# An attention block in which one shifted copy of VectorE's exponentials is made by accumulating DMA transfers

## The chip, the cores and the metric

The kernel runs on one core of one Trainium2 chip. Its time is the device time of one launch, in microseconds (us). Five engines work side by side: PE (TensorE, matmuls), ACT (ScalarE), DVE (VectorE), POOL (GpSimd) and SP (SyncE, which here only issues DMA transfers). Each engine has its own queue and runs it in order; they wait for one another through semaphores.

## The reference

Multi-head attention with 16 heads of 28 columns, for one sequence of 2048 positions and a width of 448, in bf16:

```python
qkv = (x @ wqkv).reshape(B, S, 3, H, Dh).transpose(2, 0, 3, 1, 4)
q, k, v = qkv[0], qkv[1], qkv[2]
scores = einsum("bhqd,bhkd->bhqk", q, k) * (Dh ** -0.5)
p = softmax(scores, axis=-1)
o = einsum("bhqk,bhkd->bhqd", p, v)
return o.transpose(0, 2, 1, 3).reshape(B, S, D) @ wo
```

## The kernel before, in words

**Tiling.** The 16 heads form 4 groups `g` of 4, a head taking 32 partitions. The 2048 queries form 4 chunks `c` of 512. A pair (g, c) is a set, so there are 16 sets, and in each set every head has 16 key tiles of 128 keys: 64 steps a set, 1024 in all. In a step PE multiplies keys by queries into 128x512 scores in PSUM (L706), an engine takes their exponential, and PE multiplies the values by it into the set's bank `o` (L994). A ones column in V gives the softmax's denominator. When a set is complete, VectorE copies `o` to `o_sb` (L1023), SyncE gathers the denominators into `den`, VectorE takes reciprocals (L1032), SyncE scatters them to DRAM (`scr`) and spreads them over partitions (`rr`, L1042), and POOL multiplies `o_sb` by `rr` (L1045). The output projection follows for a chunk that has all four groups.

**Two ways to the exponential.** ACT takes two steps at a time from a pair of banks (`a0`, `a1`): one 128x1024 Exp into a bf16 tile `pt` (L898; ten such tiles, NPT). VectorE takes one step at a time from a bank `d0`, `d1` or, when free, `m`. Scores come scaled by 128 times log2 e, so that adding a constant and storing int16 gives the bits of a bf16 number near the exponential (L913, tile `I`). Its error is averaged out by two further copies, the same integers plus 43 and plus 85 (SHIFT), `J1` and `J2`, which meet copies of V scaled by 201/256 and 159/256. Four VectorE steps form a chain: one `I` tile of 128x2048, and when it is complete, VectorE adds 43 and then 85 to the whole tile (two instructions of L936). So a step of VectorE has three value matmuls, and one of ACT's has one.

**The order.** All instructions are written out by a planner that runs when the kernel is built (`pick_pe`, `pick_act`, `pick_dve`, `pick_pool`, `pick_sp`). It keeps a time for each engine, takes the engine that is free first and gives it the best work that is ready by planned durations and latencies; each engine's queue has that order on the chip. PE puts scores first, then value matmuls in waves of four (one for each head) and side jobs: projections of K, Q and V for later groups, norms and output projections. A job has a priority, a gate (the step from which it may run), needs, and a landing time if it is a DMA. `urgent` lifts K and Q jobs of the next group when fewer than URGENT steps are left before it. If the queue of recent work is thin, PE gets a matmul of zeros (`dense`).

**VectorE's share.** `d_more` gives VectorE a step whenever it has a free bank and `dve_ok` finds that VectorE will be done by the time ACT runs out of what is left; otherwise ACT takes it. A chain opens for the current set, or for the next one when the current set has fewer than 2*DRAIN steps left. There may be NCH = 3 chains with value matmuls still to come.

**POOL and VectorE.** `port` keeps a planned POOL job and a planned J pass (or other VectorE pass from SBUF to SBUF) apart, and `after_shared` makes each POOL job wait for the last such VectorE pass ahead of it in the plan. POOL has no job that waits for a DMA other than the row scaling, and no transfers behind the head.

**Side jobs that the change touches.** `k_job` and `kn_job` (keys and their largest norm), `q_job` (a query chunk, and the SP transfers of its rows into QP, L448), `qn_job` (a bound from the query norms, two VectorE passes `z` and `su`, L502 and L505, and its SP transfers, L513), `v_job` (V projection in two parts), `oproj_job` (output rows through `osb`). Group 0 takes its weights from `WG`, two small tiles of their own; `offs` is a constant tile of two rows which SP copies into all QP tiles at the start (L184).

Of the kernel before, what the change touches and what calls it, by code (L numbers as in the profile page):

```python
# [12 lines left out]
I16 = mybir.dt.int16  # L13
# [11 lines left out]
URGENT = 100  # L25
# [3 lines left out]
class Op:  # L29
    def __init__(self, eng, dur, emit, need=(), gives=(), pri=0, acq=None, rel=None, gate=0, lag=0.0, land=0.0,  # L30
                 cols=0, port=False):
        self.eng, self.dur, self.emit = eng, dur, emit
        self.need, self.gives, self.pri = list(need), list(gives), pri
        self.acq, self.rel, self.gate, self.lag, self.land, self.cols, self.port = acq, rel, gate, lag, land, cols, port
# [3 lines left out]
def kernel(  # L38
# [35 lines left out]
    NCH = 3  # L74
    DRAIN = 8
# [20 lines left out]
    WG = [big.tile([CK, CC, HG * Dh + WPAD], BF16, name=f"WG{t}") for t in range(2)]  # L96
# [31 lines left out]
    def load_w0(t, eng):  # L128
        eng.dma_start(out=WG[t][:], in_=wq3[:, :, t * D:t * D + HG * Dh + WPAD])
# [33 lines left out]
    offs = const.tile([2, QW], BF16, name="offs")  # L163
# [12 lines left out]
    nc.vector.memset(offs[:], OFFS)  # L176
# [4 lines left out]
    for z in range(2):  # L181
        for c in range(NQC):
            for k in range(2):
                nc.sync.dma_start(out=QP[c][k][z][HP * k + Dh + NQC - 1 - c:P:2 * HP, :], in_=offs[:])  # L184
# [67 lines left out]
    def run(op, t):  # L252
        op.emit()
        if op.eng == "PE":
            note(t, op.cols)
        end = t + op.dur
        if op.eng == "PE" and main_on():
            cur["c_end"] = end
        if op.port:
            port[op.eng] = end  # L260
        for n in op.gives:
            evt[n] = (end + op.land, op.eng)
        if op.acq is not None:
            res[op.acq] = None
        if isinstance(op.rel, tuple):
            parts.setdefault(op.rel[0], []).append(end + LATS.get((op.eng, "PE"), LAT))
            if len(parts[op.rel[0]]) == op.rel[1]:
                res[op.rel[0]] = max(parts.pop(op.rel[0]))
        elif op.rel is not None:
            res[op.rel] = end + LATS.get((op.eng, "PE"), LAT)  # L270
        ops[op.eng].remove(op)
        return end
# [59 lines left out]
    def kn_job(g, bank, pri, gate=0):  # L332
        key = ("KN", g)

        def mm(sc):
            if sc == 0:
                held[key] = bank_tile(bank) if bank[0] != "a" else pair_tile(bank)
            quarters(held[key][:, 0:QW], maskK[:, sc, :], sqt.pop(("K", g, sc))[:], sc == 0, sc == NQC - 1)

        def red():  # L340
            kst[g] = wk.tile([P, 1], F32, name="kst")
            nc.vector.reduce_max(out=kst[g][:], in_=held.pop(key)[:, 0:QW], axis=AX.X)

        def spread_rows():
            a = wk.tile([P, HP], F32, name="kbc")
            nc.vector.tensor_copy(out=a[:], in_=kst[g][:].to_broadcast([P, HP]))
            b = wk.tile([P, HP], F32, name="kbt")
            nc.vector.transpose(out=b[:], in_=a[:])
            kmt[g] = wk.tile([P, 1], F32, name="kmt")
            cur["shared"] = nc.vector.reduce_max(out=kmt[g][:], in_=b[:], axis=AX.X)  # L350

        for sc in range(NQC):
            add("PE", D_WAVE, lambda sc=sc: mm(sc), pri=pri, gate=gate, cols=512,
                need=[("ksq", g, sc)] + ([("KNp", g, sc - 1)] if sc else []), gives=[("KNp", g, sc)],
                acq=bank if sc == 0 else None)
        add("DVE", 0.61, red, need=[("KNp", g, NQC - 1)], gives=[("kst", g)], rel=bank, pri=pri)
        add("DVE", 0.65, spread_rows, need=[("kst", g)], gives=[("km", g)], pri=pri, port=True)
# [66 lines left out]
    def q_job(g, c, bank, pri, gate=0, split=2):  # L424
# [9 lines left out]
        def evac():  # L434
            if first:
                t = qtt[0] = wk.tile([P, QW], BF16, name="qt0", bufs=1)
            else:
                t = QAt[(g, c)] = big.tile([P, QW], BF16, name=f"QA{c}", tag=f"QA{c}", bufs=1)
            if first:
                nc.vector.tensor_scalar(out=t[:], in0=held[key][:, 0:QW], scalar1=qmask[:, 0:1],  # L440
                                        scalar2=qoff[:, 0:1], op0=ALU.mult, op1=ALU.add)
            else:
                nc.vector.tensor_copy(out=t[:], in_=held[key][:, 0:QW])  # L443
# [12 lines left out]
        if first:  # L456
            add("ACT", 0.62, lambda: act_square(key, qmask), need=[key + (split - 1,)], gives=[("qsq", g, c)],
                rel=(bank, 2), pri=pri)
        else:
            add("POOL", 1.08, lambda: square(key, QAt[(g, c)][:]), need=[key], gives=[("qsq", g, c)], pri=pri, port=True)  # L460
            add("SP", 2.4, rows, need=[key, ("QZ", c, g % 2)] + ([("Oset", ORDER.index((g - 2, c)))] if g > 1 else []),
                gives=[("QR", g, c)], land=1.6, pri=1)
# [29 lines left out]
    def qn_job(g, cs, bank, pri, gate=0):  # L492
# [15 lines left out]
        def place():  # L508
            su = held.pop(("su",) + key)
            for c in cs:  # L510
                for k in range(2):
                    r = slice(HP * k + Dh + c, P, 2 * HP)
                    nc.sync.dma_start(out=QP[c][k][g % 2][r, :], in_=su[r, :])  # L513

        for k in range(len(cs)):
            add("PE", D_WAVE, lambda k=k: mm(k), pri=pri, gate=gate, cols=512,
                need=[("qsq", g, cs[k]), ("km", g)] + ([key + (k - 1,)] if k else []), gives=[key + (k,)],
                acq=bank if k == 0 else None)
        add("DVE", 0.88, bound, need=[key + (len(cs) - 1,)], gives=[("su",) + key], rel=bank, pri=pri, port=True)
        add("SP", 1.2 * len(cs), place, need=[("su",) + key] + [("QR", g, c) for c in cs],  # L520
            gives=[("QA", g, c) for c in cs], land=1.4, pri=1)

    def v_job(g, b, t0, bank, pri, gate=0, eng="DVE"):

        key = ("V", g, b, t0)
        n = XB if g is not None else XB // 2
        g0, g1 = (g, g + 1) if g is not None else (GH, G)
        w = (g1 - g0) * HG * Dh

        def mm(part):  # L530
            if part == 0:
                held[key] = bank_tile(bank)
            for u in range(part * n // 2, (part + 1) * n // 2):
# [15 lines left out]
        for p in range(2):  # L549
            add("PE", 4 * 0.1 if g is None else 8 * 0.065, lambda p=p: mm(p), pri=pri, gate=gate, cols=4 * 196,  # L550
                need=[("XT", b, 0), ("XT", b, 1), ("W", 2)] + ([key + (p - 1,)] if p else []), gives=[key + (p,)],
                acq=bank if p == 0 else None)
        add(eng, 0.53 if eng == "DVE" else 0.5, evac, need=[key + (1,)],
# [12 lines left out]
    def oproj_job(c, tq, pri):  # L566
# [8 lines left out]
        def evac():  # L575
            held[key + ("sb",)] = osb = wk.tile([P, D], BF16, name="osb", bufs=4)
# [9 lines left out]
        add("DVE", 0.535, evac, need=[key + (1,)], gives=[key], rel="m", pri=pri)  # L586
        add("SP", 0.4, store, need=[key], gives=[key + ("st",)], pri=9)
# [62 lines left out]
    for g in range(1, G):  # L650
# [4 lines left out]
        jobs += [lambda gt, c=c: q_job(g, c, "m", 100 * g + 10 + c, gt) for c in range(NQC)]  # L655
        jobs += [lambda gt: qn_job(g, list(range(NQC)), "m", 100 * g + 20, gt)]
# [20 lines left out]
    chain = {"cur": None, "used": 0}  # L677
# [70 lines left out]
    def dve_ok(t, k):  # L748
        if chain["cur"] is None and chain["used"] >= NCH:
            return False  # L750
        if chain["cur"] is not None and half_left(chain["cur"]["s"], 0) != half_left(chain["cur"]["s"], 1):
            return True
        fin = max(free["DVE"], t + 0.5) + 0.62 * (len(a_fifo) + k + 1) + 1.4 + (1.2 if adds else 0.0)
# [30 lines left out]
    def d_more(s, t, acting):  # L784
        got, taken = [], []
        for b in d_banks(t):
# [8 lines left out]
            if ch is None:  # L795
                chain["used"] += 1
                ch = chain["cur"] = {"I": wk.tile([P, HG * QW], I16, name="I4", bufs=NCH), "s": step[0], "n": 0,
                                     "open": 0, "next": 0, "done": 0}
# [111 lines left out]
    def do_a(t):  # L910
# [6 lines left out]
        ch["open"] += NTERM  # L917
        ch["done"] += 1
        pending.append({"step": step, "k": 0, "ap": dst.bitcast(BF16), "ready": end + LATS[("DVE", "PE")], "pt": None, "ch": ch})
        if ch["done"] == HG:  # L920
            adds.append([ch, HG, 1])
        else:
            flush()
        return end

    def flush():
        ch = chain["cur"]
        if ch is not None and ch["done"] == ch["n"] and not any(remain[ch["s"]]):
            chain["cur"] = None
            adds.append([ch, ch["n"], 1])  # L930

    def do_add(t):
        ch, m, k = adds[0]
        w = slice(0, m * QW)
        r = ch[k] = wk.tile([P, HG * QW], I16, name=f"J{k}", bufs=NCH)
# [16 lines left out]
    def pv_cands(t):  # L952
# [6 lines left out]
        for e in pending:  # L959
            if e["step"][0] == s and e["ready"] <= t:  # L960
                v = v_time(e)
                if v is not None and v <= t:
                    out_.append(e)
        return out_
# [14 lines left out]
    def do_pv(t, ws):  # L979
# [9 lines left out]
        for w in ws:  # L989
# [7 lines left out]
            for e in w:  # L997
# [5 lines left out]
                else:  # L1003
                    e["ch"]["open"] -= 1
                    if e["ch"]["open"] == 0 and e["ch"] is not chain["cur"] and e["ch"]["done"] == e["ch"]["n"]:
                        chain["used"] -= 1
# [4 lines left out]
    def finish_set(s, end):  # L1011
# [9 lines left out]
        def evac():  # L1021
            st["o_sb"] = wk.tile([P, QW], F32, name="o_sb")
# [16 lines left out]
        def spread():  # L1039
            scr = st["scr"]  # L1040
            st["rr"] = wk.tile([P, QW], F32, name="rr")
# [6 lines left out]
        add("DVE", 0.61, evac, need=[("Oset", s)], gives=[("osb", s)], rel="o", pri=-5)  # L1048
        add("SP", 0.6, gather, need=[("osb", s)], gives=[("den", s)], land=1.5, pri=2)
        add("DVE", 0.16, recip, need=[("den", s)], gives=[("rec", s)], pri=50, lag=2.0, port=True)  # L1050
        add("SP", 0.35, scatter, need=[("rec", s)], gives=[("scr", s)], land=1.1, pri=2)
        add("SP", 0.5, spread, need=[("scr", s)], gives=[("rr", s)], land=7.0, pri=2)
# [21 lines left out]
    def urgent(op):  # L1074
        n = op.gives[0]
        if n[0] not in ("K", "KNp", "Q", "QN") or n[1] == 0:
            return False
        first = min(k for k in range(NSET) if ORDER[k][0] == n[1])
# [52 lines left out]
    def pick_dve(t):  # L1131
        flush()
        op, nxt = best("DVE", t)
        can_add = adds and port["POOL"] <= t
# [6 lines left out]
        if op is not None:  # L1141
            return run(op, t), None
        if a_fifo and a_fifo[0][0] <= t:
# [4 lines left out]

    def pick_pool(t):
        op, nxt = best("POOL", t)  # L1150
        if op is not None:
# [92 lines left out]
    for tq in rest:  # L1244
# [4 lines left out]
        osb = wk.tile([P, D], BF16, name="osb", bufs=4)  # L1249
# [35 lines left out]
```

## Time and profile before

| what | value |
|---|---|
| median of 3 runs | 366.55 us (366.45 to 366.99) |
| profiled execution | 366.38 us, its span 364.6 us |
| first and last exponential of L898 start | 19.0 us, 355.2 us |
| J passes (L936): shortest, median, longest | 630, 686, 1401 ns |
| copies of `o` (L1023), one a set | 44.5 us the first, 337.2 us the last |
| ACT waits of PE for a score bank (L706 behind L898) | 10.0 us in 29 waits |
| PE waits for QP rows by DMA | 0.8 us in 2 waits |
| mean DMA rate over the span | 34 GB/s |

The span runs from the first to the last instruction; the time of an execution has a little around it. In a row of a group stand the line, engine, operation, output and input, shapes and count, then the busy time, the mean of one alone, the idle time just before such instructions and what ended it.

### The profile page before, as it was taken

How to read it: one execution, taken by the hardware profiler on the slowest of the kernel's cores; microseconds unless marked ns; L12 is line 12 of the kernel's file. 1: busy time of each engine (PE TensorE's matmuls, PEld its weight loads, DVE VectorE, ACT ScalarE, POOL GpSimd, SP SyncE). 2: the span in 40 equal slices, each digit the busy share in tenths (PEclk: the TensorE clock that was granted, in tenths of full speed). 3: DMA queues.
4: the chain of work that ended last, by engine and by line, in shares of the span. 5: the costliest groups of instructions: out<-in, count | busy, mean ns of one | idle time of the engine just before them, and what ended most of it. 6: DMA issues, size and time to landing. Idle time of an engine off the chain costs nothing.

```text
span 364.6 us, 10984 instructions
## 1 busy us (share of the span) xinstructions
PE 346.3 (95%) x4515; PEld 115.5 (32%) x4515; DVE 343.8 (94%) x646; ACT 347.7 (95%) x381; POOL 68.0 (19%) x103
## 2 busy tenths in 40 slices
PE   8999999999999999999999999998998999999995
PEld 4433233332333333332222322222322232222233
DVE  7789998999999999999999998999999999999993
ACT  4789999999999999999999999999999999999992
POOL 8941113013102212212012223101010010101010
PEclk9999999999999999999999999999999999999999
DMA  8520100001110000011000001100000001010111
GB/s 238 141 46 15 28 14 22 4 32 24 31 34 30 4 5 31 17 31 39 18 16 3 31 10 37 43 19 13 4 30 3 32 13 55 16 60 24 41 44 52
DMA packets 15050, 12.30 MB, mean 34 GB/s; under 512 B 6808, under 2 KB 13080, under 8 KB 15000
## 3 DMA queue, kind: packets, MB, share of 16 engines
q1 hardware_dynamic: 13448, 10.18, 9.9%
q10 hardware_dynamic: 1040, 1.02, 0.9%
q8 instruction: 35, 0.57, 0.7%
q0 software_dynamic: 512, 0.40, 0.5%
q14 instruction: 15, 0.12, 0.1%
HBM read 7.58 MB, written 1.96 MB: 26 GB/s over the span
## 4 chain that ended last, share of the span: by engine, by line
PE 53%; ACT 32%; issue 7%; DVE 6%; DMA 1%; DVEq 0%; ACTq 0%
ACT pt L898 32%; PE a L706 20%; PE o L994 15%; PE m L282 7%; PE m L289 7%; DVE I L913 2%; DVE J L936 1%; DMA xs<-in_x_dram 1%; PE a L282 1%; PE d L282 1%; DVE QA L443 0%; PE o L738 0%; PE d L289 0%; PE d L706 0%; ACT L146 0%
## 5 line engine op out<-in xcount | busy, mean ns | idle before, releaser
L898 ACT ACTIVATE pt<-a 128x1024 bf16<-128x1024 f32 x366 | 336.4, 1186 | 1.7 <-PE d L706 0.8
L913 DVE TENSOR_SCALAR I<-d 128x512 int16<-128x512 f32 x264 | 173.4, 683 | 7.3 <-PE d L706 6.5
L706 PE MATMUL a<-QP,KA 32*128 32x512 bf16 (+1 forms) x720 | 140.9, 381 | 11.4 <-ACT pt L898 10.0
L994 PE MATMUL o<-pt,V 128*32 128x512 bf16 x732 | 107.2, 384 | 0.1
L936 DVE TENSOR_SCALAR J<-I 128x2048 int16<-128x2048 int16 x146 | 98.5, 699 | 0.3
L706 PEld LDWEIGHTS <-KA 32*128 32x128 bf16 (+1 forms) x1041 | 51.0, 91 | 149.4 <-issue 146.5
L706 PE MATMUL d<-QP,KA 32*128 32x512 bf16 (+1 forms) x259 | 85.7, 384 | 0.0
L994 PE MATMUL o<-J,V 128*32 128x512 bf16 x584 | 79.0, 384 | 0.0
L994 PE MATMUL o<-I,V 128*32 128x512 bf16 x292 | 66.4, 385 | 0.2
L994 PEld LDWEIGHTS <-V 128*32 128x32 bf16 x1608 | 29.4, 94 | 48.9 <-issue 45.9
L1045 POOL TENSOR_TENSOR xs<-o_sb,rr 128x512 bf16<-128x512 f32 x12 | 15.3, 1273 | 107.6 <-DVE J L936 80.1
L282 PE MATMUL m<-XT,WRAW 112*32 112x512 bf16 x384 | 29.8, 384 | 0.0
L304 POOL TENSOR_TENSOR sq<-QA 128x512 bf16<-128x512 bf16 x15 | 15.6, 1040 | 57.6 <-DVE QA L443 28.7
L304 POOL TENSOR_TENSOR sq<-KA 128x512 bf16<-128x512 bf16 x12 | 12.5, 1039 | 60.0 <-DVE KA L322 34.8
L913 DVE TENSOR_SCALAR I<-m 128x512 int16<-128x512 f32 x28 | 19.1, 683 | 0.0
L289 PE MATMUL m<-WRAW,XT 112*32 112x112 bf16 (+1 forms) x768 | 18.1, 230 | 0.0
L1045 POOL TENSOR_TENSOR OTL<-o_sb,rr 128x512 bf16<-128x512 f32 x3 | 3.8, 1272 | 57.5 <-DVE J L936 57.5
L289 PEld LDWEIGHTS <-XT 112*32 112x32 bf16 x768 | 11.7, 96 | 8.1 <-issue 8.1
L289 PE MATMUL m<-WO,xs 128*32 128x448 bf16 x156 | 12.1, 358 | 0.0
L1023 DVE COPY o_sb<-o 128x512 f32<-128x512 f32 x15 | 10.3, 686 | 0.9 <-PE o L994 0.6
L289 PE MATMUL m<-sq,maskK 128*32 128x512 bf16 x108 | 10.8, 388 | 0.3 <-DVE QA L443 0.2
L706 PE MATMUL m<-QP,KA 32*128 32x512 bf16 (+1 forms) x28 | 10.8, 384 | 0.0
(113 smaller groups left out, 192.1 us busy)
## 6 DMA issues: line engine op xcount, KB each, us to landing
rr<-scr SPq DMA_DIRECT2D x15, 256.0 KB
QP<-QA SPq DMA_DIRECT2D x60, 28.0 KB
out_dram<-osb SPq DMA_DIRECT2D x12, 112.0 KB
WRAW<-in_wqkv_dram SPq DMA_DIRECT2D x3, 392.0 KB
xs<-in_x_dram ACTq DMA_DIRECT2D x4, 224.0 KB
xs<-in_x_dram SPq DMA_DIRECT2D x4, 224.0 KB
QP<-su SPq DMA_DIRECT2D x32, 2.0 KB
out_dram<-pt SPq DMA_DIRECT2D x2, 224.0 KB
```

Source lines behind the costliest of these rows:

```text
L282: nc.tensor.matmul(out=ps[HP * i:HP * (i + 1), :], lhsT=w[:, cc, h * Dh:h * Dh + HP], rhs=XT[c][cc // 2][:, cc % 2, :], start=(cc == 0), s ...
L289: nc.tensor.matmul(out=out[r, :], lhsT=lhsT[:, r], rhs=rhs, start=start, stop=stop, tile_position=(0, HP * i), **k)
L304: after_shared(nc.gpsimd.tensor_tensor(out=t[:], in0=src, in1=src, op=ALU.mult))
L706: nc.tensor.matmul(out=out_ap, lhsT=KAt[(g, j // XB)][r, (j % XB) * P:(j % XB + 1) * P], rhs=q[r, :], start=(n == 0), stop=(n == len(terms ...
L898: nc.scalar.activation(out=pt[:], in_=ps[:], func=ACT.Exp, scale=LN2 / 128.0)
L913: nc.vector.tensor_scalar(out=dst, in0=pd[:], scalar1=BIAS, scalar2=0.0, op0=ALU.add, op1=ALU.max)
L936: cur["shared"] = nc.vector.tensor_scalar(out=r[:, w], in0=ch["I"][:, w], scalar1=float(SHIFT[k]), scalar2=None, op0=ALU.add)
L994: nc.tensor.matmul(out=o[HP * i:HP * (i + 1), :], lhsT=VT[e["k"]][g, j // XB][:, j % XB, HP * i:HP * (i + 1)], rhs=e["ap"], start=(SETMM[k ...
L1023: nc.vector.tensor_copy(out=st["o_sb"][:], in_=o[:])
L1045: m = nc.gpsimd.tensor_tensor(out=otile(g, c), in0=st["o_sb"][:], in1=st["rr"][:], op=ALU.mult)
```

## The change

**J1 of an early chain by DMA.** If a chain opens with at least FAR = 30 steps left in its set, and the set isn't the first (FIRST = 1), it is "far": POOL fills its `J1` tile with 43 in every int16 ahead of time (a memset of 128x1024 int32 words), and when the chain's `I` is complete, POOL issues a DMA transfer that adds `I` to `J1` (`accum_op=ALU.add`). VectorE's first J pass is left out for it; the pass for `J2` stays. Other chains keep both passes. The plan has 1.05 us for the fill, 0.88 for the issue and ACC_LAND = 5.6 for the landing, and for 1.5 us behind the planned landing PE takes such blocks last.

**Buffers.** `I4` has four tiles (NCH), `J1` four (NJ), `J2` three (NCH2), each with a test of its own on what has used it; before, all three had three. Room comes from `WG` (now in the `rr` and `o_sb` buffers), `offs` (now in a `pt` tile, an exponential's), `qt0` (now in `z`), one `rr` instead of two, three `osb` instead of four, and one `kbc` and `kbt` each.

**The plan.** SyncE's transfers get longer landings (QP rows 4.0 for later groups where 1.6 stood, bounds 5.0 for 1.4, `den` 3.0 for 1.5, `rr` 8.0 for 7.0, output stores 5.0). DRAIN is 10 instead of 8. V jobs have four parts instead of two and count as urgent (URGENT_V); URGENT is 130; the later part of a started job counts as urgent. The bound job of group 1 is split, chunk 0 by itself; transfers of bounds are planned chunk by chunk. A chain that has waited AGE = 2.5 for its J pass goes ahead of passes from PSUM, and POOL may give way to it once in 3 us.

```diff
-URGENT = 100
+URGENT = 130
+URGENT_V = 40
...
-    NCH = 3
-    DRAIN = 8
+    NCH = 4
+    NCH2 = 3
+    NJ = 4
+    FAR = 30
+    FIRST = 1
+    AGE = 2.5
+    SPLITQ = {1: ([0], [1, 2, 3]), 2: ([0, 1, 2, 3],), 3: ([0, 1, 2, 3],)}
+    ACC_LAND = 5.6
+    DRAIN = 10
...
-    offs = const.tile([2, QW], BF16, name="offs")
+    offs = wk.tile([P, 2 * QW], BF16, name="pt", bufs=NPT)[0:2, 0:QW]
...
-        if chain["cur"] is None and chain["used"] >= NCH:
-            return False
+        if chain["cur"] is None and len(chain["all"]) >= NCH:
+            old = chain["all"][-NCH]
+            if not j1_free() or not used_up(old, 0) or any(a[0] is old for a in adds) or old["acc"] is None or old["acc"] > t:
+                return False
...
+                ch[1] = wk.tile([P, HG * QW], I16, name="J1", bufs=NJ)
+                if sum(len(q) for q in remain[step[0]]) >= FAR and step[0] >= FIRST:
+                    ch["far"] = True
+                    far_chain(ch)
...
+    def far_chain(ch):
+        n = len(chain["all"])
+        fill = SHIFT[1] * 65537
+
+        def emit():
+            m = nc.gpsimd.memset(ch[1][:].bitcast(I32), fill)
+            after_shared(m)
+
+        ch["id"] = n
+        add("POOL", 1.05, emit, gives=[("fill", n)], pri=20, port=True)
+
+    def accumulate(ch, m):
+        w = slice(0, m * QW)
+        ch["acc"] = None
+
+        def emit():
+            after_shared(nc.gpsimd.dma_start(out=ch[1][:, w], in_=ch["I"][:, w], accum_op=ALU.add))
+
+        def landed(end):
+            at = ch["acc"] = end + ACC_LAND
+            for n in range(m):
+                pending.append({"step": ch["steps"][n], "k": 1, "ap": ch[1][:, n * QW:(n + 1) * QW].bitcast(BF16),
+                                "ready": at, "pt": None, "ch": ch})
...
+        out_.sort(key=lambda e: bool(e["ch"] and e["ch"]["far"] and e["k"] == 1 and t < e["ready"] + 1.5))
...
-        add("SP", 0.5, spread, need=[("scr", s)], gives=[("rr", s)], land=7.0, pri=2)
+        add("SP", 0.5, spread, need=[("scr", s)], gives=[("rr", s)], land=8.0 if s < NSET - 2 else 6.0, pri=2)
...
+        if can_add and t > adds[0][0]["at"] + AGE:
+            return do_add(t), None
```

## The prediction

> **What bounds the kernel now.** I read the busy table first, then the costliest groups, then busy time by stage.
>
> ```profile
> PE 346.3 (95%) x4515; PEld 115.5 (32%) x4515; DVE 343.8 (94%) x646; ACT 347.7 (95%) x381; POOL 68.0 (19%) x103
> ```
> Three engines are near full at once, so the average alone names none. The groups tell them apart:
>
> ```profile
> L898 ACT ACTIVATE pt<-a 128x1024 bf16<-128x1024 f32 x366 | 336.4, 1186 | 1.7 <-PE d L706 0.8
> L913 DVE TENSOR_SCALAR I<-d 128x512 int16<-128x512 f32 x264 | 173.4, 683 | 7.3 <-PE d L706 6.5
> ...
> L936 DVE TENSOR_SCALAR J<-I 128x2048 int16<-128x2048 int16 x146 | 98.5, 699 | 0.3
> ```
> Ahead of the exponentials ACT stood idle for 1.7 us in all. They run from 18.97 to 356.4 us: 366 of 336.4 / 366 = 0.919 us (busy time over count; 1186 ns is one alone, they overlap). So span = 19.0 head + 366 x 0.919 + 1.0 gaps + 8.2 tail = 364.6. The profiled execution took 366.38, that is 1.78 around the span, and lies 0.17 under the median of 366.55. **The time falls only if there are fewer exponentials**, 0.919 us for each, and one is two of the 1024 (head, key tile) steps: 366 x 2 = 732 are ACT's and 264 + 28 (the `m` row) = 292 VectorE's. VectorE is as full: a step costs it (173.4 + 19.1) / 292 = 0.66 us, and each chain of four steps two J passes of 98.5 / 146 = 0.675. The split stands where both run out together. PE follows by stage (columns: window, length, then busy time and count of PE, PEld, DVE, ACT, POOL):
>
> ```profile
> 43.00:158.00 115.00, 114.08 (x1648) 38.64 (x1644) 111.81 (x203) 115.00 (x127) 21.63 (x20) 1.00 0.08 21
> 158.00:181.00 23.00, 21.54 (x256) 7.05 (x254) 22.64 (x41) 22.97 (x26) 2.59 (x3) 1.00 0.10 26
> 181.00:227.00 46.00, 44.98 (x514) 13.14 (x515) 43.17 (x74) 46.00 (x51) 10.82 (x10) 1.00 0.08 21
> 227.00:342.00 115.00, 107.13 (x1196) 32.46 (x1189) 112.94 (x190) 114.64 (x126) 7.63 (x6) 1.00 0.08 26
> ```
> Up to 158 us PE has 0.9 us free, behind 227 us 7.9 us. The granted clock (third column from the end) is 1.00 throughout, so it takes no part.
>
> **What goes from VectorE.** Chains are 292 / 4 = 73, or 4.6 in each of 16 sets. A chain becomes "early" when at least 30 of its set's 64 steps are left (none in the first set). The next set's first chain may open when fewer than 20 steps of the current one are left. ACT needs 10 x 0.919 = 9.2 us for those 20; VectorE needs about 4 x 0.66 + 1.35 = 4.0 us a chain, 4.6 with its other work. So two chains open early, and then each chain sees 4 steps of its own and 10 of ACT's go by: openings at 64, 60, 56, 42 and 28 left. Four of 4.6 qualify; a full set of buffers will refuse some, so I take 3.5 (bounds 3 to 4), or 52 chains in 15 sets. VectorE loses 3.5 x 0.675 = 2.36 us of work per set.
>
> **What that is worth at most.** A step moved from ACT costs VectorE 0.66 + 0.675 / 4 = 0.83 us and shortens the period by 0.46, which VectorE loses too: 2.36 / (0.83 + 0.46) = 1.83 steps, a period shorter by 0.84 us of 21; over 15 sets -12.6 us.
>
> **What PE takes back.** A step on VectorE has three value matmuls where ACT's has one. Four side by side start 0.22 us apart (137.82 and 138.05 in the timeline), so 1.83 steps add 3.66 / 4 x 0.22 = 0.20 us; with the shorter period PE must find 1.04 us in each set. Its room is idle time plus the zero matmuls that fill it. To 227 us, 8.8 sets, that is 0.9 + 1.5 + 1.0 idle and 2.0 of zeros: 5.4 us where 9.2 are wanted, and I count 40% of the gain there (filling every gap would be 58%): 8.8 x 0.84 x 0.4 = 3.0. Behind 227 us the room is 7.9 + 8.4 over 5.5 sets, 3.0 a set: all of it, 6.2 x 0.84 = 5.2. Sum -8.2. Splitting the V projection in four instead of two changes no matmul, only where one fits; that and the urgency limits stand behind my taking 40% and not the 16% that the first five sets alone would give.
>
> **What POOL takes on.** Each early chain brings a fill of 128x1024 words and one transfer issue. The nearest rows are the V memset of 128x1024 (1.03 us) and the 16 WO issues:
>
> ```profile
> L205 POOL DMA_DIRECT2D WO<-in_wo_dram x16: 505/505/690, 13.9 to 21.5; - x16
> ...
> DMA to landing us min/median/max: 1.9/2.2/3.5
> ```
> Those issues have 28 rows, these 128: between 0.5 us and 128 / 28 x 0.5 = 2.3; I take 0.9, nearer to the one row. 52 x 1.93 = 100 us on an engine busy for 43 of the 335 us behind the head: it has the room, but what stands in its queue (squares for K and Q, the row scaling, the next fill) waits while the transfer's issue waits for the chain's last pass. POOL now idles up to 19 us between jobs, so this is hidden. What isn't free is VectorE's side:
>
> ```profile
> 250.59 1.27 POOL L1045 TENSOR_TENSOR xs<-o_sb,rr 128x512 bf16<-128x512 f32 x1 [14.80 <-DVE J L936]
> ```
> ```profile
> 250.43 0.69 DVE L913 TENSOR_SCALAR I<-d 128x512 int16<-128x512 f32 x1
> 251.03 1.39 DVE L936 TENSOR_SCALAR J<-I 128x2048 int16<-128x2048 int16 x1
> ```
> The pass from PSUM runs beside POOL undisturbed (0.69), the J pass waits until POOL is done at 251.86 and needs 0.56 more. Four such collisions (124, 224, 251 and 271 us) cost 0.1 + 0.4 + 0.7 + 0.6 = 1.8 us. Were starts random, 146 passes against POOL's 13% would wait 146 x 0.13 x 0.55 = 10.4 us; the planner avoids five sixths. After: 52 of some 153 passes are gone, 101 x 0.43 x 0.5 = 22 at random, a fifth of it 4.4: 2.6 more, at 0.46 / 1.29 of a microsecond each +0.9. The Trainium skill ("SBUF — State Buffer", section "Who interferes with whom") says of this that the shared port pair is an exclusive lock which the first holds for its whole instruction; the trace agrees (0.69 became 1.39). Its section "SBUF: two separate sides" adds, against this change, that descriptors issued from GpSimd can't be written while VectorE holds the pair; no row here shows an issue beside a J pass.
>
> **The transfer's landing.** 512 KB are read twice and written once. Below: 2.2 us (WO, 24.5 KB). Above: a `rr` spread of 256 KB was used 5.0 us behind its issue's end (229.51 to 234.52); four times its part beyond 2.2 gives 13. Between: in the first 20 us the engines, 0.68 busy, moved 178 GB/s, so 262 when full; two passes of 512 KB are 4.0, with 2.2 some 6.2 us. I take that. The plan allows 0.88 + 5.6 and asks for these blocks last for 1.5 us more, so PE, which runs in written order, then waits for none: 0 us. The bounds stay for the rivals.
>
> **The rest.** A second bound for group 1's queries: z and su, 0.75 + 0.29, 1.0 us of VectorE, +0.4 by the same ratio. A longer way from I to J, with J2 queued behind POOL's longer holds: some VectorE gaps, +0.5, an estimate (the row for gaps before L913 shows 7.3 in all). The constant rows in an exponential's tile: last read issued at 18.8 us, and that tile returns ten exponentials later, 28 us: 0. First weights in `rr` and `o_sb`: last read at 37 us, first rewrite at 44.5: 0. One `rr` buffer for one spread in 21 us: 0; three output buffers: stores start in the last 70 us, one each 1.5 at the densest, 0 (+0.5 if a store lands late). SyncE's queue: the same transfers in number, due later in the plan; the trace has 0.8 us of PE waiting for QP rows, so at most -0.8; I take 0, since transfers get neighbours. Sum: -8.2 + 0.9 + 0.4 + 0.5 = **-6.4**, on the median 366.55: **360.1 us** (its own range 356.5 to 364).
>
> **Rivals.**
> - PE has no room before 227 us: only the late 5.2 stay, less 1.8: 363.2. For it: 0.9 free in 115 us. Against: the work there is placed by spread-out gates, not by need. 0.12.
> - All of it converts, projections moving into the late gaps: -12.6 + 1.8: 355.8, or 354 with 4 chains a set. 0.10.
> - The port: by full exclusion and random starts J passes wait 22 us, 20 more than now, (35 - 20) of 35 us are left: -12.6 x 0.43 + 1 is 362 where PE allows it, 364 where it gives 60%. For it: 1.39 us above. Against: written-out order. 0.08. By the skill's rule of exclusion this would hold for issues too.
> - The gain is eaten by VectorE waiting for fills and buffers: within 0.2%, which is 0.7 us, about what a measurement of this kernel can tell from no change. 0.05.
> - **Slower**: transfers land later than planned. PE's queue is in order, so each early chain can stall PE, with it the scores and ACT. From 0.12 us mean stall (6.4 / 52) the gain is gone; at 0.3 us it is 360.1 + 15.6 = 375.7. It decides where landing passes 6.5 + 1.5 = 8 us from the issue's start. For it: the bound of 13, and the row spreads and QP rows on the same engines. Against: the busy share of DMA is 0.08. 0.19.
>
> Forecast 0.46. Faster 0.46 + 0.12 + 0.10 + 0.08 = 0.76, same 0.05, slower 0.19. From 354 to 370 us lies all but most of the slower case (0.13 of 0.19) and a little of the fast one.
>
> **What would show it.** About 359 exponentials (366 - 6.4 / 0.919) and 306 VectorE steps; near 101 J passes by VectorE; 52 fills and 52 issues on POOL; PE idle before the value matmul for J of less than 5 us to DMA; PE's idle behind 227 us roughly halved. Wrong if exponentials fall and the time doesn't (stalls: see who ends ACT's idle), if fewer than 40 chains qualify, or if the J passes' mean rises above 0.75.

## The result, and the profile after

The changed kernel takes 365.13 us (median of 20 runs, 363.21 to 368.74), the kernel before 366.65 us (20 runs, 366.28 to 366.99). The ratio is 0.9953, 95% interval 0.9936 to 0.997: faster by 0.5%, where 1.8% was forecast (360.1 us, 356.5 to 364 for the likeliest case). One of the 20 runs, the one of 368.74 us, was in a slower state of the chip and is left out of the ratio; the other 19 have a median of 364.88 us, which stands for the change where runs are compared below. The profiled execution took 365.38 us, its span 363.5.

The groups of the changed kernel that bear on the forecast, to be laid beside those of before:

```profile
L924 ACT ACTIVATE pt<-a 128x1024 bf16<-128x1024 f32 x358 | 329.5, 1134 | 3.6 <-PE d L726 2.5
L939 DVE TENSOR_SCALAR I<-d 128x512 int16<-128x512 f32 x279 | 182.1, 681 | 9.9 <-PE d L726 8.5
...
L986 POOL DMA_DIRECT2D J<-I x57 | 52.1, 915 | 76.7 <-DVE I L939 55.2
L1069 PE MATMUL o<-J,V 128*32 128x512 bf16 x616 | 80.2, 386 | 4.0 <-DMA J<-I 4.0
L975 POOL MEMSET J<- 128x1024 int32 x57 | 60.3, 1064 | 48.7 <-DVE J L1010 17.8
L1010 DVE TENSOR_SCALAR J<-I 128x2048 int16<-128x2048 int16 x97 | 72.3, 758 | 0.2
```

There are 358 exponentials instead of 366 and 308 VectorE steps instead of 292; 57 chains go by transfer. So the exchange took place as forecast (359 and 306, 52 chains; 308 are the 279 above and 29 on bank `m`), and the exponentials' busy time fell by 336.4 - 329.5 = 6.9 us. But the span fell by 1.1. A sum of four terms shows where the rest went (first exponential's start; busy; gaps between; from the last one's end to the span's end):

| | head | exponentials | gaps | tail | span |
|---|---|---|---|---|---|
| before | 19.0 | 336.4 | 1.0 | 8.2 | 364.6 |
| changed | 18.9 | 329.5 | 3.1 | 12.0 | 363.5 |

2.1 us came back as gaps and 3.8 us in the tail. The new words in the groups are "DMA J<-I": PE now waits for transfers to land. The answer for the line of the issues (L986) says how long landings take, from issue to landed (first line: who waited for them, for how many us, how often):

```profile
  PE o L1069: 4.0, 3
...
DMA to landing us min/median/max: 4.4/4.9/8.7
```

The median is below the 6.2 us that I had put; the longest is above the 8 us from which I had said that landings decide. The answer covers 43 of the 57 transfers; the trace also keeps, for all of them, the 16 completion marks that each leaves one by one. By these three took more than 8 us and all others at most 6.5: those issued at 251.07 us (8.5), 253.73 (8.4) and 343.84 (8.7). PE's three waits are for these three; the last two are in the chain that ended last. In the timeline stand start, duration, engine, line, operation, and in brackets the idle time before it and who ended it; its last three lines are from the last set:

```profile
259.58 0.40 PE L1069 MATMUL o<-J,V 128*32 128x512 bf16 x4 [0.54 <-DMA J<-I]
...
262.18 0.39 PE L1069 MATMUL o<-J,V 128*32 128x512 bf16 x1 [1.34 <-DMA J<-I]
...
343.84 0.86 POOL L986 DMA_DIRECT2D J<-I  x1 [2.29 <-DVE osb L593]
...
350.09 0.40 PE L1069 MATMUL o<-J,V 128*32 128x512 bf16 x4
352.58 0.62 PE L1069 MATMUL o<-J,V 128*32 128x512 bf16 x4 [2.10 <-DMA J<-I]
```

PE's next matmul in its queue is the one for the last `J1`, so it stands still for 2.1 us, and the value matmuls of ACT's last exponentials stand behind it. And the four matmuls behind the wait take 0.62 us where 0.40 stood before it. The windows say why (window, length, busy of PE, PEld, DVE, ACT, POOL, then granted clock, DMA share, GB/s):

```profile
350.00:352.00 2.00, 0.49 (x6) 0.10 (x4) 0.00 (x0) 1.55 (x2) 0.93 (x1) 1.00 0.20 44
352.00:354.00 2.00, 1.42 (x16) 0.66 (x20) 0.00 (x0) 0.00 (x0) 0.00 (x0) 0.52 0.01 3
```

The granted clock falls to 0.52 behind the gap. The other thing to see is the DMA share of 0.20 while PE waits: most of the 16 engines are idle, about three still work. The transfer isn't short of total bandwidth; a few engines are late. The marks show which part: of the transfers issued at 251.07 and 253.73 us twelve marks came 4.3 to 4.6 us behind the issue and four 8.3 to 8.5 us behind it; of the one at 343.84 eleven by 4.7, one at 6.2 and four at 7.7 to 8.7.

**The theory (L).** At 340.78 us SyncE had issued the spread of reciprocals, `rr<-scr`: 256 KB whose source is 4 rows, each repeated 32 times. If a few engines carry all of it, an accumulating transfer, spread over all 16, is complete only when its share on those few has come through. At 251.07 and 253.73 the same stands ahead of it: a spread at 250.73. Before the change PE hardly ever waited for a transfer in the steady part (0.8 us for QP rows). **Rivals:** VectorE's J passes hold back POOL's descriptors (P); the last set's end costs the time by its place, whatever lands when (T).

### The profile page after: what moved, and what is told of

Same layout as the page of the kernel before. It is cut to its first block, busy times and chain, and to the rows that moved or that the text cites. A ratio compares the mean times of both kernels' runs of the same rounds, so it can differ in the third digit from the quotient of the medians.

```text
span 363.5 us, 11157 instructions
## 1 busy us (share of the span) xinstructions
PE 339.5 (93%) x4500; PEld 110.4 (30%) x4500; DVE 333.4 (92%) x615; ACT 340.8 (94%) x373; POOL 174.8 (48%) x217
## 4 chain that ended last, share of the span: by engine, by line
ACT 39%; PE 30%; DVE 15%; issue 8%; DMA 6%; POOL 0%; DVEq 0%; ACTq 0%
ACT pt L924 38%; PE a L726 11%; PE o L1069 8%; DVE I L939 6%; DMA J<-I 5%; PE m L301 5%; DVE J L1010 3%; PE m L294 3%; DMA xs<-in_x_dram 1%; DVE KA L334 1%; DVE V L575 1%; DVE V L562 1%; DVE QA L456 1%; PE a L294 1%; PE d L301 1%
## 5 line engine op out<-in xcount | busy, mean ns | idle before, releaser
L924 ACT ACTIVATE pt<-a 128x1024 bf16<-128x1024 f32 x358 | 329.5, 1134 | 3.6 <-PE d L726 2.5
L939 DVE TENSOR_SCALAR I<-d 128x512 int16<-128x512 f32 x279 | 182.1, 681 | 9.9 <-PE d L726 8.5
L726 PE MATMUL a<-QP,KA 32*128 32x512 bf16 (+1 forms) x704 | 137.2, 381 | 12.3 <-ACT pt L924 11.4
L726 PE MATMUL d<-QP,KA 32*128 32x512 bf16 (+1 forms) x274 | 96.8, 383 | 0.0
L726 PEld LDWEIGHTS <-KA 32*128 32x128 bf16 (+1 forms) x1041 | 46.0, 91 | 146.2 <-issue 144.8
L986 POOL DMA_DIRECT2D J<-I x57 | 52.1, 915 | 76.7 <-DVE I L939 55.2
L975 POOL MEMSET J<- 128x1024 int32 x57 | 60.3, 1064 | 48.7 <-DVE J L1010 17.8
L1010 DVE TENSOR_SCALAR J<-I 128x2048 int16<-128x2048 int16 x97 | 72.3, 758 | 0.2
L301 PE MATMUL m<-WRAW,XT 112*32 112x112 bf16 (+1 forms) x768 | 20.7, 230 | 0.3 <-DVE KA L334 0.3
L456 DVE CAST QA<-m 128x512 bf16<-128x512 f32 x15 | 10.3, 685 | 1.1 <-PE m L294 1.1
```

What stands on the lines that cost most here:

```text
L301: nc.tensor.matmul(out=out[r, :], lhsT=lhsT[:, r], rhs=rhs, start=start, stop=stop, tile_position=(0, HP * i), **k)
L726: nc.tensor.matmul(out=out_ap, lhsT=KAt[(g, j // XB)][r, (j % XB) * P:(j % XB + 1) * P], rhs=q[r, :], start=(n == 0), stop=(n == len(terms ...
L924: nc.scalar.activation(out=pt[:], in_=ps[:], func=ACT.Exp, scale=LN2 / 128.0)
L939: nc.vector.tensor_scalar(out=dst, in0=pd[:], scalar1=BIAS, scalar2=0.0, op0=ALU.add, op1=ALU.max)
L975: m = nc.gpsimd.memset(ch[1][:].bitcast(I32), fill)
L986: after_shared(nc.gpsimd.dma_start(out=ch[1][:, w], in_=ch["I"][:, w], accum_op=ALU.add))
```

## The experiments

Times are medians; ratios are of means, against the kernel before, run on the same chip. Runs 1, 2, 4 and 7 were on one chip (kernel before 366.53 us), the others on another (366.40 us for runs 5, 6, 8 and 9).

**1. The spread in four transfers**, one for each head; the planner isn't told, so each engine has the same order of work.

```diff
-            nc.sync.dma_start(out=st["rr"][:], in_=scr[:].unsqueeze(1).to_broadcast([HG, HP, QW]))
+            for i in range(HG):
+                nc.sync.dma_start(out=st["rr"][HP * i:HP * (i + 1), :], in_=scr[i:i + 1, :].to_broadcast([HP, QW]))
```

> The changed kernel with one edit: the spread of the reciprocals into rr is issued as four transfers of 32 partitions, one for each head, instead of one whose slowest dimension is 4; the planner's figures are left, so every engine has the same order of work. Theory L (a few accumulating transfers land late because the rr spread holds a few of the 16 DMA engines for long, and PE stands behind them): in the changed kernel the DMA share while PE waited for the last transfer was 0.20 (350 to 352 us), so most engines were already done; with the spread divided, the longest landing falls from 8.7 to about 6 us, PE's waits for transfers of J (9.0 us with the weight loads') fall under 3 us, the clock stays at 1.00 and the time falls by 3 to 5 us, to 360 to 362. Rival P (the late ones were late because VectorE's J passes kept POOL's descriptors back): landings and time as in the changed kernel, 365 us. Rival T (the end of the last set costs the time whatever lands): 365 us. The Trainium skill (DMA: Bandwidth & Descriptors, section Why a DMA increments its semaphore by 16 and not by 1) states that a transfer goes to the largest number of engines up to 16 that divides its slowest dimension, which would be 4 for the one spread and 16 for each of the four.

Measured: 360.61 us (360.28 to 361.05), ratio 0.9839, interval 0.9827 to 0.9852. Its groups, and its line of landings:

```profile
L924 ACT ACTIVATE pt<-a 128x1024 bf16<-128x1024 f32 x358 | 329.4, 1138 | 2.1 <-PE a L726 1.1
...
L1069 PE MATMUL o<-J,V 128*32 128x512 bf16 x616 | 80.0, 384 | 0.2 <-DMA J<-I 0.2
```
```profile
DMA to landing us min/median/max: 4.4/4.9/6.3
```

The same 358 exponentials, the same median landing; only the longest are gone (6.3 for 8.7; by the marks of all 57, 6.4), and PE's wait for transfers with it. The granted clock is 1.00, gaps are 1.5 us and the tail 9.0. This edit alone gives 4.3 us (360.61 against 364.88), more than twice what the whole change had given, and the time is 0.5 us from the forecast. The late landings are the cause; that leaves T without work to do. The edit does one thing more: `rr` itself lands sooner, so POOL's row scaling, which had waited 9.0 us for it in four places, waits for it no longer. That isn't what PE had stood behind: its transfers were late counted from their own issue, and the two long waits of POOL, 3.2 and 5.0 us, ended at 257.8 and 349.7 us, behind those issues. Why the transfers were late, the next run says.

**2. Landings by themselves.** No attention; each case six times, one after the other. `gate` lets VectorE read what has landed and then write `I` and `rr`, which releases the next case.

```python
for n in range(N):
    gate(r=True)
    spread_one()
    nc.gpsimd.dma_start(out=J1[:], in_=I[:], accum_op=ALU.add)
```

> No attention is computed (the output is zeros): six times each, one after the other, an accumulating transfer of 512 KB alone; beside eight J passes of VectorE; beside one rr spread; beside the spread in four transfers; two accumulating transfers together; and both spreads alone. Its time means nothing, only the landings. All theories: alone 4.5 to 5 us. Theory L: beside the one spread about 8 us, beside four transfers about 6; beside J passes within 1 us of alone. Rival P: beside J passes 7 us or more, beside either spread the same, at most 6.

Measured, from issue to landing (in this order: alone; beside eight J passes; beside the one spread; beside four transfers; the first and the second of two together):

```profile
DMA to landing us min/median/max: 4.5/4.5/5.3
DMA to landing us min/median/max: 4.9/4.9/5.0
DMA to landing us min/median/max: 8.2/8.2/8.5
DMA to landing us min/median/max: 4.9/4.9/5.1
DMA to landing us min/median/max: 4.5/4.6/4.6
DMA to landing us min/median/max: 6.6/6.6/6.8
```

One spread adds 3.7 us, the same bytes in four transfers 0.4, and eight back-to-back J passes 0.4. The J passes lengthen the issue (1.27 us instead of 0.86), not the landing by much: P falls. DMA's share in the case of the one spread shows the tail again:

```profile
80.00:84.00 4.00, 0.00 (x0) 0.76 (x1) 1.00 0.67 139
84.00:88.40 4.40, 0.00 (x0) 0.00 (x0) 1.00 0.23 52
```

0.23 of 16 engines are 3.7: for the last four microseconds about four engines work and twelve are done. The marks of this transfer say the same: twelve at 4.3 to 4.5 us, four at 8.2 to 8.5, as in the kernel. In the case of the four transfers all 16 of the first come between 4.6 and 5.0 us.

**3. How many engines, or how many transfers?** Four transfers differ from one in both. So: two transfers of two heads, and one transfer whose source has 16 rows repeated 8 times.

```python
def spread_two():
    for i in range(2):
        nc.sync.dma_start(out=rr[64 * i:64 * (i + 1), :], in_=scr[2 * i:2 * i + 2, :].unsqueeze(1).to_broadcast([2, HP, QW]))

def spread_wide():
    nc.sync.dma_start(out=rr[:], in_=scw[:].unsqueeze(1).to_broadcast([16, 8, QW]))
```

> No attention is computed (the output is zeros): six times each, an accumulating transfer of 512 KB beside the one spread, beside the spread in two transfers of two heads, and beside one transfer of the same 256 KB whose source has 16 rows, each repeated 8 times, instead of 4 repeated 32 times; then the last two spreads alone. Theory K (the number of engines follows from the slowest dimension, and a few engines carry the whole spread): beside the one spread 8.2 us again; two transfers go to 2 engines, so beside them 10 us or more, and alone more than the 4.8 of the one spread; the 16-row transfer goes to 16 engines, so beside it 5 us, and alone about 3.4 us. Rival N (many small transfers land faster because they interleave): two transfers 6 to 7 us, the 16-row transfer 8 us as the one spread.

Measured beside the one spread, two transfers, and the 16-row transfer:

```profile
DMA to landing us min/median/max: 5.2/8.2/8.4
DMA to landing us min/median/max: 9.2/9.3/9.3
DMA to landing us min/median/max: 5.1/5.1/5.3
```

(The shortest, 5.2 us, is the first of its six; its spread was issued 11 us later.) Alone, two transfers need 8.0 us, the 16-row one 3.1 to 3.4, the one spread (run 2) 4.8. More transfers made it worse, and one transfer with 16 rows is as good as four. The marks count the late engines: beside the one spread four of the 16 come behind 8.0 us, beside two transfers two (9.1 to 9.3 us, the other 14 by 4.6), beside the 16-row transfer none (all between 4.6 and 5.3). So the count of rows in the slowest dimension sets how many engines carry the bytes, and two transfers of two rows use the same two (9.3 where I had put at least 10: the size was a little off). The Trainium skill ("DMA: Bandwidth & Descriptors", section "Why a DMA increments its semaphore by 16 and not by 1") says just that, the largest number up to 16 that divides the slowest dimension of both sides; the 8.2, 9.3 and 5.1 us for 4, 2 and 16 agree.

**4. No accumulating transfers in the last set.**

```diff
-                if sum(len(q) for q in remain[step[0]]) >= FAR and step[0] >= FIRST:
+                if sum(len(q) for q in remain[step[0]]) >= FAR and FIRST <= step[0] < NSET - 1:
```

> The changed kernel without accumulating transfers in the last set (chains there keep both J passes on VectorE); the plan is the same up to the last set's first chain. Theory L: the wait of 2.1 us for the last transfer and the half clock behind it (0.50 to 0.53 from 352 to 355 us) go, some 3.8 us, and the last set has about 2 exponentials more (1.8 us): 362.5 to 363.5, and less spread from run to run. Rival T (the last set ends late by itself): 365 to 367. Rival P gives the same as L here, since the last set then has no transfer to keep back.

Measured: 364.29 us (363.51 to 366.49), 0.9939 (0.9925 to 0.9953), against 0.9953 (0.9936 to 0.997) for the change: intervals that overlap, so no gain is shown, and above the 362.5 to 363.5 that L had. The profiled execution, the longest of the six, shows both parts. The tail is 8.0 us where the change had 12.0, so the wait for the last transfer and what followed it are gone as L had it; the 360 exponentials cost 2.3 us more. But the stall near 262 us is still there (from 250 to 264 us ACT is busy for 12.0 of 14, clock 0.96), here with a half clock of 6.8 us behind it, and the gaps are 5.4 us where they were 3.1. Other runs of the six, with a clock of 1.00, took 363.5 to 364.2 us.

**5. Runs 1 and 4 together.**

> The changed kernel with the spread in four transfers and no accumulating transfers in the last set. Theory L: with landings near 5 us the last set's transfers cost nothing any more, so to leave them out only costs: about 360 exponentials where the spread alone had 358, 2 x 0.92 = 1.8 us, and VectorE idle at the end: 362 to 363.5 us. Rival T (the last set's transfers cost by their place at the end, however fast): below 360.6.

Measured: 362.06 us (361.80 to 362.65), 0.988 (0.9865 to 0.9895); 360 exponentials. Slower by 1.45 us than run 1 (by 1.5 going by the ratios), as L had it, and not below 360.6 as T had it: nothing here says that the last set's transfers cost by their place. Run 1 had taken T's ground already. That these transfers are worth having is likely from this but not shown, since run 9 shows as large a difference between two plans.

**6. The kernel before with the divided spread.**

> The kernel before with the spread of the reciprocals in four transfers of 32 partitions, and nothing else; same order of work. Theory L says that the single spread harms only the accumulating transfers beside it, and there are none here: 366.3 to 366.8 us, no change. If the four transfers help by themselves (POOL's row scaling earlier, QP rows earlier), it would be 361 to 364, and the gain of the run with both would not be the landing's.

Measured: 366.66 us, 1.0006 (0.9997 to 1.0015). The edit gives nothing by itself; its 4.3 us exist only where something waits for transfers beside the spread.

**7. No chain by transfer, all other edits kept.**

```diff
-    FAR = 30
+    FAR = 999
```

> The changed kernel with no chain far at all (the limit of steps left set to 999): the plan's other edits, the buffers and the SyncE landings stay, no fills, no accumulating transfers. All theories have the gain of the exponentials in the transfers: about 366 exponentials and 365.5 to 367.5 us. If the other edits carry part of the gain, it is below 365; if they cost, above 368, and the transfers gain more than the whole change shows.

Measured: 365.98 us, 0.9997 (0.9978 to 1.0015), 366 exponentials. The other edits (buffers, SyncE's landings, the split jobs) are worth nothing that can be measured together; the gain of the change is the transfers'. (The profiled execution was its slowest, 369.7 us, which raises the mean and so the ratio; the other nine lie at 365.75 to 366.81.)

**8. More chains by transfer, with the divided spread.** Run 1's edit is in this run too; the diff shows what is added to it.

```diff
-    FAR = 30
+    FAR = 20
```

> The changed kernel with the spread in four transfers and the limit of steps left at 20 instead of 30, so that nearly all chains of sets 1 to 15 go by transfer. VectorE loses some 12 more passes of 0.67 us, 8 us, worth 8 x 0.46 / 1.29 = 2.9 us of exponentials at most; but a chain opened with 20 left closes some 10 steps before its set's end, 10 x 0.33 = 3.3 us, and its transfer needs 0.9 + 4.9: the set's last wave waits. Expected: 360 to 364, with PE's waits for J above 3 us; 358 would say the landing is hidden there too.

Measured: 361.82 us (361.77 to 362.08), 0.9873 (0.9858 to 0.9887): in the range, but not for the reason given. 71 transfers, 356 exponentials, and PE and its weight loads wait at most 1.9 us for J: the landing is hidden there too. Against run 1 the exponentials' busy time is 0.9 us less, but gaps are 3.0 us where they were 1.5, and the tail 9.8 where it was 9.0: there output blocks were left to the end in this plan (a copy of ACT at 356.9 us, the last store issued at 357.4). Why the plan has the gaps, and no place for the blocks sooner, wasn't tried.

**9. The plan told of the divided spread.** Run 1's edit is in this run too.

```diff
-        add("SP", 0.5, spread, need=[("scr", s)], gives=[("rr", s)], land=8.0 if s < NSET - 2 else 6.0, pri=2)
+        add("SP", 1.8, spread, need=[("scr", s)], gives=[("rr", s)], land=5.0, pri=2)
```

> The changed kernel with the spread in four transfers and its planned figures set to them: 1.8 us of issue and 5.0 of landing instead of 0.5 and 8.0 (6.0 for the last sets). The plan changes in many places. Output projections can be written earlier; the exponentials' number is set by VectorE's share and should stay near 358: 359.5 to 361.5 us, within the scatter of replanning.

Measured: 362.97 us (362.83 to 363.01), 0.9902 (0.9885 to 0.9918), with 358 exponentials and 61 transfers: above the expected range. Better figures made a plan that is 2.4 us worse. Of this, 1.1 us are in the tail (10.1 where run 1 has 9.0; the same late output block, copied at 357.75 us), 0.7 in gaps and 0.6 in the exponentials' busy time; what in the plan makes them stays open. It shows how far two plans of nearly equal content lie apart, and so that differences of 1 to 2 us between runs 1, 5, 8 and 9 are no ground for ranking their ideas. Run 1 is the fastest version of all.

## Why the prediction was wrong, point by point

- **What bounds the kernel: right, but not the whole sum.** An exponential costs 0.92 us in all runs, whether 366, 358, 360 or 356 of them. But their number alone doesn't order the versions: the change, run 1 and run 9 all have 358 and lie 4 us apart, most of it in gaps and tail, which the forecast had left at 1.0 and 8.2 us.
- **How many chains, how many exponentials: right.** 57 chains (52, bounds 45 to 60), 358 exponentials (359), 308 VectorE steps (306), 97 J passes (101). Fill 1.06 us and issue 0.92 (1.03 and 0.9).
- **PE's room: right in sum, a little off by stage.** Run 1 has the plan without the stalls. The copies of `o` for the ninth set start at 213.63 us before and 211.75 in run 1, those of the 15th at 337.24 and 330.70. Up to the ninth copy 1.9 us were won where 3.0 were counted (before what the port and the rest take back), and 4.7 in the six sets after it, 0.78 a set where 0.84 were. But the sign named for it didn't come: from 227 to 342 us PE is idle for 9.0 us in run 1, where 7.9 stood and half of it was expected, and its matmuls of zeros fell from 8.8 us (8.4 in the forecast, a slip in adding) to 4.8. So the size came out, in part by luck; that PE's room sets it isn't shown.
- **The port: under-sized, but without effect on the end.** A J pass costs 72.3 / 97 = 0.745 us where it cost 0.675; 97 x 0.07 is 6.8 us of VectorE's time instead of the 2.6 put. VectorE bore it with the gaps that the plan left it (busy 333.4 of 363.5 us), and the exponentials' number isn't moved by it, since it is fixed when the plan is made. The sign "J passes' mean above 0.75" hangs on the reading: the mean of one alone is 0.758 us, the busy time over the count 0.745.
- **The transfer's landing: the step that failed.** It said "PE, which runs in written order, then waits for none: 0 us". The typical landing was shorter than estimated (4.9 for 6.2; the upper bound's 5.0 us for a spread ran from its issue's start, and POOL had then been waiting for VectorE, not for the spread). But I worked with one figure for all, and took DMA's busy share of 0.08 as evidence against lateness. That was the share before the change; the transfers themselves raise it to 0.55 (43 to 227 us) and 0.64 (227 to 342). And a share is a mean over 16 engines; a spread on four of them leaves it low and still keeps a quarter of an accumulating transfer waiting. PE waited in three places, 4.0 us in all. The sign "less than 5 us to DMA" was met, and was set too wide: these 4.0 us, with the clock, are where the gain went. Between the profiled executions of the change and of run 1 lie 4.7 us of span: 1.6 of gaps and 3.0 of tail, of which 2.1 are the wait and some 0.6 the half clock behind it (from the second wave of that `J1` to the copy of `o` 2.3 us instead of 1.7); 0.3 stay unexplained.
- **The slower rival** named this mechanism, with 8 us as the point from which it decides. That point was right: the three transfers above 8 us stalled PE, and in run 1, with 6.4 us at most, PE waits 0.2 us. But it was priced as a mean over all 52 chains and given 0.19 as a case by itself. It was neither all nor none: three waits, behind three of 57 transfers, took some 70% of the gain (4.3 us by run 1, of 5.9). A term of 1 to 5 us in the sum, with a look at which transfers run beside a spread, would have put the forecast at 361 to 365.
- **The tail**: 8.2 us before, 9.0 in run 1. 0.8 us that I hadn't counted: for most of it, twelve output matmuls (at 352.61 us) now stand between the last set's scaling and its own output, where before they ran earlier, beside the copy of `o` (356.63). That run 1 comes within 0.5 us of the forecast is in part luck too: one exponential fewer than forecast (-0.9) offsets this.

## What to carry to other kernels

When work moves to a transfer that an in-order queue waits for, don't ask for its mean landing but for its longest, and for what shares its engines at that moment; list the transfers that run on few engines, by their slowest dimension, before anything else. A low DMA share doesn't exclude it: here 0.20 with PE waiting meant that a few engines were late. A small repair beside the change (here the shape of an old transfer that cost nothing before) can be worth more than the change.

## What the runs showed of the hardware that was not expected

- In a gap of 2.1 us in PE's work the granted clock fell to 0.50, from 352.07 to 355.48 us, so for 3.4 us. The Trainium skill ("TensorE: Matmul & The Clock Gate", Part 1) gives an idle window of about 3.4 us; here less was enough, and the measurement decides. Less than 2.1 can be enough too: in run 4 a gap of 1.30 us (0.96 us of idle shortly before it) brought 6.8 us of half clock from 262.97 us, and in run 7 one of 1.23 us at 26 us brought 3.4 us of it. In the changed kernel one of 1.34 us at 261 us (0.54 before it) left the clock at 1.00. What decides between them isn't shown.
- The change's runs scatter with the clock: of the 19, those with a mean clock of 0.998 or more took 363.2 to 364.1 us, those with 0.991 or less 366.0 to 367.2. Run 1, at 0.998 to 1.000, took 360.3 to 361.1: so with the clock whole the late landings cost about 3 us, and where it falls up to 3 more.
- An accumulating transfer of 512 KB from SBUF to SBUF lands 4.5 us behind its issue alone (run 2); of two issued 0.6 us apart the first needs 4.6 us and the second 6.6, each from its own issue.
- Eight VectorE passes from SBUF to SBUF back to back delayed the landing of such a transfer by only 0.4 us (run 2).
